# All of w_mod loaded at the start of a decode layer, the last weights behind the last V tile

## The chip, the cores and the metric

The kernel runs on one core of a Trainium2 chip. The metric is the device time of one execution in microseconds (us). Before the change it is 397.99 us, the median of three runs (397.88 to 398.57). The times in the rows further down come from one profiled execution.

## The reference

One decode step of a transformer layer for 8 sequences, all in 32-bit floats. Six vectors per sequence are computed from a conditioning input `c` and scale, shift and gate the two halves of the layer.

```
mod = (silu(c) @ w_mod).reshape(8, 6, 1, 512)
sa, ca, ga, sb, cb, gb = mod[:, 0], ..., mod[:, 5]
h = layernorm(x) * (1 + ca) + sa
q = (h @ wq)                      # 32 heads of 128, 4 heads share one of 8 KV heads
p = softmax(q k^T / sqrt(128))    # over the last 2048 of 8192 cached keys
x = x + ga * ((p v) @ wo)
h = layernorm(x) * (1 + cb) + sb
h = h @ w1 + b1                   # 512 -> 1792
x = x + gb * (relu(h)**2 @ w2 + b2)
```

## The kernel before, in words

The kernel reads some 165 MB once: 64 MiB of K, 64 MiB of V, 8 MiB each of `wq` and `wo`, 6 MiB of `w_mod`, 3.5 MiB each of `w1` and `w2` (1 MiB is 1.05 MB). All these loads are issued by one engine, SyncE (SP), in the order of the list `loads` (L144 to L152). Each goes into a slot of SBUF: two big slots (4 MiB, K tiles above all) and five small ones (2 MiB, V tiles and weights). `pump` issues the next load of the list as soon as a slot of its size is free; `done` frees one. An issue that waits holds back all those behind it, since SP works in order.

A K tile holds the 2048 keys of four sequences for one KV head; there are 16 (K0 to K15), and each head needs two. A V tile holds the values of two sequences for one head; there are 32 (V0 to V31). The main loop (L501) has one step per V tile, `s`: in a step TensorE (PE) transposes half a K tile (`transposes`, L222), multiplies the transposed keys by the queries (`scores`), and multiplies the softmax weights by a V tile that is five steps back (`weighted`, L442). VectorE (DVE) and ScalarE (ACT) copy the transposed tiles out of PSUM. Every fourth step ends a head: `soft_a` to `soft_d` do its softmax, `gather` (L471) brings the head's output into columns, and `project_o` (L486) multiplies it by the rows of `wo` for that head and adds up in `wo_ps`.

Before the loop stands the head of the program: `modulation` (L253) with the first third of `w_mod` (`modA`: sa, ca), the first layer norm, and `project_q` (L314). Of `wq` the first four heads are computed before the loop, the other four at step 4.

Behind the loop stands the tail, one long chain: `at_i` (the attention output, out of `wo_ps`), `modulation` again with the other two thirds of `w_mod` (`modB`, L117, loaded in two pieces), the residual `x1`, the second layer norm, the products with `w1` (L594), the squared relu `rT`, the products with `w2` (L614), the last two VectorE operations (L622, L623), and the output's transfer. One product that nobody reads (L611, into `spin_ps`) stands ahead of those with `w2`. The loads behind V31 are `modB`, the two biases, `w1` and `w2`.

Of the kernel before, what the change touches and what calls it, by code (L numbers as in the profile page):

```python
# [20 lines left out]
def tile_adaln_cached_attention_mlp(  # L21
# [65 lines left out]
    def size_of(key):  # L87
        return "big" if key[0] in ("K", "modB") or key == ("wo", HKV // 2 - 1) else "small"

    def load(key):  # L90
# [7 lines left out]
        if kind in "KV":  # L98


            if kind == "K":
                v = k_cache[4 * (i % 2) : 4 * (i % 2) + 4, i // 2]
            else:
                v = v_cache[i % C :: C, i // C]
            v = v[:, SK - W :, :].rearrange("u (p j) d -> p u (j d)", p=P // v.shape[0])
            nc.sync.dma_start(t, v)
            return
        if kind == "wo":

            r = 2 * REP * DH  # L110
            v = wo[i * r : (i + 1) * r, :].rearrange("(h p i) n -> p h (i n)", p=P, i=4)
        elif kind == "modA":
            v = w_mod[:, : 2 * D].rearrange(r_kc, p=P)
        elif kind == "modB":
            v = w_mod.rearrange(r_kc, p=P)
            for lo, hi in ((2, 5), (5, 6)):
                nc.sync.dma_start(  # L117
                    t[:, NQ * D * (lo - 2) : NQ * D * (hi - 2)].rearrange("p (a n) -> p a n", a=NQ),
                    v[:, :, D * lo : D * hi],
                )  # L120
            return
# [100 lines left out]
    def transposes(q, g, e):  # L222
# [30 lines left out]
    def modulation(wms, nq):  # L253

        pm = ps_m.tile([P, 512], F32, name="m_ps", tag="m_ps")
        for kc in range(NQ):
            wv = wms[kc].rearrange("p (m q n) -> p m q n", m=nq, q=NQ)
            for q in range(NQ):
                nc.tensor.matmul(
                    pm[32 * q : 32 * q + 32, : nq * P].rearrange("p (m n) -> p m n", m=nq),  # L260
                    cT[:, kc, :],
                    wv[:, :, q, :],
                    start=(kc == 0),
                    stop=(kc == NQ - 1),
                )
        return pm[:, : nq * P].rearrange("p (m n) -> p m n", m=nq)

# [16 lines left out]
    modA = consts.tile([P, 2, P], F32, name="modA")  # L284
    m = slot(("modA", 0), 2 * D)
    pm = modulation([m[:, kc, :] for kc in range(NQ)], 2)
    done(("modA", 0))
    nc.vector.tensor_copy(modA[:, 0, :], pm[:, 0, :])
    nc.vector.tensor_scalar(modA[:, 1, :], pm[:, 1, :], 1.0, None, op0=ALU.add)
# [19 lines left out]
    nc.vector.scalar_tensor_tensor(h, h, rstd, modA[:, 0, :], op0=ALU.mult, op1=ALU.add)  # L309
    hT = consts.tile([P, NQ, 32], F32, name="h1T")  # L310
    to_columns(h, hT)
    transposes(0, 1, 1)

    def project_q(r, between=()):  # L314
        pq = ps_m.tile([P, 512], F32, name="m_ps", tag="m_ps")
        for kc in range(NQ):
            w = slot(("wq", 2 * r + kc // 2), 2048)
            for g in range(4):
                nc.tensor.matmul(  # L319
                    pq[32 * g : 32 * g + 32, :],  # L320
                    hT[:, kc, :],
                    w[:, kc % 2, 512 * g : 512 * g + 512],
# [3 lines left out]
            if kc % 2:  # L326
                done(("wq", 2 * r + kc // 2))
                if between:
                    transposes(*between[kc // 2])
        qs = work.tile([P, 512], F32, name="qs", tag="a", bufs=1)  # L330
        nc.scalar.copy(qs, pq)
# [8 lines left out]
    project_q(0, ((0, 2, 0), (0, 2, 1)))  # L340
# [320 lines left out]
```

## Time and profile before

| what | value |
|---|---|
| median of three runs | 397.99 us |
| the profiled execution: its own time | 399.03 us |
| the profiled execution: span from first to last instruction | 397.2 us |
| PE busy | 327.0 us (82%) |
| DVE busy | 179.1 us (45%) |
| ACT busy | 97.0 us (24%) |
| read from HBM | 164.77 MB, 415 GB/s over the span |
| mean granted clock of TensorE | 0.974 of full speed |

The busy share is an average over the whole run. What a change is worth is read from the stage where it acts, from what each engine waits for there. "Critical chain" is the chain of work that ended last, followed back from the last instruction. The granted clock is 1.00 at 2.4 GHz and 0.50 at 1.2 GHz.

### The profile page before, as it was taken

To read this page: it belongs to the slowest core of one execution; us is meant where nothing else is said; L and a number is where in the kernel's file an instruction comes from. 1 tells how busy PE (TensorE), PEld (TensorE's weight loads), DVE (VectorE), ACT (ScalarE), POOL (GpSimd) and SP (SyncE) were. 2 spreads that over 40 slices of the span, in tenths; PEclk is the share of its full clock that TensorE was granted. 3 is DMA by queue.
4 is the path that set the end of the run, shared out by engine and by line. 5 is a ranking of instruction groups with operands and counts; after the bars stand their busy time and mean duration, and the time that the engine had idled before them with its cause. 6 is when DMAs were issued, how large, how long until landed. Compare 5 with 4: busy or idle time off the path is not lost.

```text
span 397.2 us, 6042 instructions
## 1 busy us (share of the span) xinstructions
PE 327.0 (82%) x2574; PEld 165.4 (42%) x2574; DVE 179.1 (45%) x417; ACT 97.0 (24%) x169; POOL 2.4 (1%) x12
## 2 busy tenths in 40 slices
PE   0477979796989968999869898998978789979574
PEld 0343535443444534444434444544444344533134
DVE  6142323553454435545623455555535364456320
ACT  1132224221222213123212232223122222230010
POOL 2000000000000000000000000000000000000000
PEclk9999999999899989999998999999999899989998
DMA  8999999999999999999999999999999999999992
GB/s 333 408 439 411 435 426 449 404 445 407 437 429 427 442 416 444 410 441 412 447 412 447 409 440 421 436 412 439 424 434 431 424 427 419 426 431 410 421 415 97
DMA packets 11867, 165.22 MB, mean 416 GB/s; under 512 B 1080, under 2 KB 1344, under 8 KB 3136
## 3 DMA queue, kind: packets, MB, share of 16 engines
q1 hardware_dynamic: 11696, 164.71, 97.7%
q8 instruction: 20, 0.33, 0.3%
q10 hardware_dynamic: 144, 0.13, 0.1%
q14 instruction: 7, 0.06, 0.0%
HBM read 164.77 MB, written 0.07 MB: 415 GB/s over the span
## 4 chain that ended last, share of the span: by engine, by line
DMA 44%; PE 41%; DVE 9%; ACT 4%; issue 1%; SPq 0%; ACTq 0%; DVEq 0%
DMA big<-in_A_k_cache_dram 33%; PE kt_ps L231 17%; PE s_ps L359 9%; PE o_ps L451 9%; DMA small<-in_B_w_dram 6%; DMA small<-in_w_mod_dram 4%; ACT pr L403 2%; DVE o_sb L467 2%; PE m_ps L475 2%; DVE kT L233 2%; DVE tr L479 1%; PE m_ps L614 1%; DVE pT L430 1%; PE m_ps L319 1%; PE m_ps L436 1%
## 5 line engine op out<-in xcount | busy, mean ns | idle before, releaser
L231 PE MATMUL kt_ps<-ident,big 128*128 128x128 f32 x1024 | 146.1, 286 | 45.9 <-DMA big<-in_A_k_cache_dram 35.8
L231 PEld LDWEIGHTS kt_ps<-ident,big 128*128 128x128 f32 x1024 | 113.0, 144 | 143.2 <-ACT kT L233 76.3
L233 DVE COPY kT<-kt_ps 128x512 f32<-128x512 f32 x128 | 88.3, 690 | 142.3 <-PE kt_ps L231 142.3
L233 ACT COPY kT<-kt_ps 128x512 f32<-128x512 f32 x128 | 74.8, 584 | 220.7 <-PE kt_ps L231 216.5
L359 PE MATMUL s_ps<-kT,qwin 128*32 128x512 f32 x512 | 71.5, 633 | 0.8 <-DVE qwin L345 0.8
L451 PE MATMUL o_ps<-small,pT 128*32 128x512 f32 x512 | 67.3, 603 | 0.1
L467 DVE SCALAR_TENSOR_TENSOR o_sb<-o_ps,diag,o_sb 128x128 f32<-128x128 f32 x96 | 33.7, 351 | 3.4
L465 DVE TENSOR_SCALAR o_sb<-o_ps,diag 128x128 f32<-128x128 f32 x32 | 11.2, 351 | 12.8 <-PE o_ps L451 12.8
L451 PEld LDWEIGHTS o_ps<-small,pT 128*32 128x32 f32 x512 | 11.1, 108 | 13.1 <-issue 11.6
L359 PEld LDWEIGHTS s_ps<-kT,qwin 128*32 128x32 f32 x512 | 10.4, 110 | 13.1 <-issue 11.4
L403 ACT ACTIVATE pr<-ss,nm 128x512 f32<-128x512 f32 x8 | 9.7, 1219 | 19.1 <-DVE nm L400 19.1
L427 PE MATMUL m_ps<-ident,pr 128*128 128x128 f32 x64 | 10.3, 289 | 2.2 <-DVE tr L479 2.2
L475 PE MATMUL m_ps<-o_sb,pick 128*128 128x512 f32 x16 | 9.3, 666 | 3.1 <-DVE o_sb L467 1.6
L427 PEld LDWEIGHTS m_ps<-ident,pr 128*128 128x128 f32 x64 | 7.7, 147 | 8.4 <-DVE tr L479 4.0
L430 DVE TENSOR_TENSOR pT<-m_ps,mine 128x512 f32<-128x512 f32 x16 | 10.4, 685 | 0.0
L371 DVE TENSOR_REDUCE mx<-ss 128x1 f32<-128x512 f32 x8 | 5.5, 687 | 8.6 <-ACT ss L369 8.5
L411 DVE COPY pr<-pr 128x512 f32<-128x512 f32 x8 | 3.4, 429 | 12.1 <-ACT pr L403 12.1
L319 PE MATMUL m_ps<-small,h1T 128*32 128x512 f32 x64 | 7.5, 597 | 1.5 <-DVE h1T L242 1.5
L369 ACT COPY ss<-s_ps 128x512 f32<-128x512 f32 x8 | 4.7, 587 | 11.5 <-PE s_ps L359 11.5
L479 DVE STREAM_TRANSPOSE tr<-m_ps 128x512 f32<-128x512 f32 x8 | 5.7, 717 | 2.5 <-PE m_ps L475 2.5
L614 PE MATMUL m_ps<-small,rT 128*32 128x128 f32 x112 | 4.8, 349 | 1.8 <-DMA small<-in_B_w_dram 1.8
L490 PE MATMUL wo_ps<-small,oT 128*32 128x512 f32 x48 | 6.2, 592 | 0.0
(124 smaller groups left out, 93.7 us busy)
## 6 DMA issues: line engine op xcount, KB each, us to landing
big<-in_A_k_cache_dram SPq DMA_DIRECT2D x16, 4096.0 KB, 23.6
small<-in_A_v_cache_dram SPq DMA_DIRECT2D x32, 2048.0 KB, 25.9
small<-in_A_wq_dram SPq DMA_DIRECT2D x4, 2048.0 KB, 35.4
small<-in_A_wo_dram SPq DMA_DIRECT2D x3, 2048.0 KB, 23.9
small<-in_B_w_dram SPq DMA_DIRECT2D x2, 1792.0 KB, 20.8
big<-in_w_mod_dram SPq DMA_DIRECT2D x1, 3072.0 KB, 22.5
small<-in_w_mod_dram SPq DMA_DIRECT2D x1, 2048.0 KB, 17.2
big<-in_A_wo_dram SPq DMA_DIRECT2D x1, 2048.0 KB
```

The lines of the kernel that those rows point to most:

```text
L231: nc.tensor.transpose(p[:, i, :], k[:, 32 * e + 8 * g + 4 * a + i, :], ident)
L233: (nc.vector.tensor_copy if a else nc.scalar.copy)(t[:, :, i : i + 4, :], p.rearrange("p i (r u) -> p u i r", u=4))
L319: nc.tensor.matmul(pq[32 * g : 32 * g + 32, :], hT[:, kc, :], w[:, kc % 2, 512 * g : 512 * g + 512], start=(kc == 0), stop=(kc == NQ - 1),)
L359: nc.tensor.matmul(s_ps[0][32 * u : 32 * u + 32, :], qwin[hk % 2][:, 4 * c + u, o : o + 32], kT[:, u].rearrange("p i r -> p (i r)"), start ...
L403: nc.scalar.activation(pr.rearrange("p i (r e) u -> p e i r u", e=2)[:, :, :, :, 0], SS_.pop(hk).rearrange("p (e i r) -> p e i r", e=2, i= ...
L427: nc.tensor.transpose(pp[:, i * P : (i + 1) * P], pr[:, 4 * a + i].rearrange("p r u -> p (r u)"), ident)
L430: nc.vector.tensor_mul(PT_[hk][:, a].rearrange("p x i r -> p i x r"), pp.rearrange("p (i x r) -> p i x r", i=4, r=2 * REP), mine.rearrange ...
L451: nc.tensor.matmul(o[32 * g : 32 * g + 32].rearrange("p j d -> p (j d)"), PT_[hk][:, h, 4 * c + g].rearrange("p i r -> p (i r)"), v[:, j : ...
L465: nc.vector.tensor_scalar(d, o[:, 0, :], diag[:, 0:1], None, op0=ALU.mult)
L467: nc.vector.scalar_tensor_tensor(d, o[:, j, :], diag[:, j : j + 1], d, op0=ALU.mult, op1=ALU.add)
L475: nc.tensor.matmul(pp, pick.rearrange("p t u -> p (t u)"), o.rearrange("p c d -> p (c d)"), start=True, stop=True)
L479: nc.vector.transpose(tr, pp.rearrange("p (c d i) -> p c i d", c=C, i=4))
```

## The change

The list of loads is put in another order, and the work that reads the moved weights moves with it.

- `w_mod` is loaded whole at the start, right behind K0, in four loads of 1.5 MiB (one row of 3072 values for each partition in each). `modulation` goes away: all six vectors are computed in the head of the program (two PSUM tiles, `pms`), and `ga`, `add`, `mul` and `modC` are kept for the tail.
- `wq` comes in four loads by rows instead of four blocks of columns, so all eight heads' queries are computed ahead of the loop; `turn_q` (copy, transposes, copy) stays in two parts, the second at step 1. V0 is loaded ahead of K2.
- The last `wo` rows leave their place among the last V tiles. They come behind V31 as two loads, in one big slot with the first half of `w1` (`tail`); `w2` gets the other big slot.
- `project_o` for head 6 moves from step 33 to the last step, next to head 7.
- The row of keys and values that a product takes is numbered another way (`16 * a + 4 * g` in place of `8 * g + 4 * a`), with the same shapes.
- `spin(n)` issues products that nobody reads: 1 behind the products `pw`, 1 ahead of `w1`, 3 ahead of `w2`, five in all where one stood.

```diff
+        elif kind == "mod":
+            rows(0, w_mod.rearrange(r_kc, p=P)[:, i : i + 1])
         elif kind == "wq":
-            r, half = divmod(i, 2)
-            v = wq[:, 2048 * r : 2048 * r + 2048].rearrange(r_kc, p=P)[:, 2 * half : 2 * half + 2]
+            rows(0, wq.rearrange(r_kc, p=P)[:, i : i + 1])
+        elif kind == "tail":
+            for h in range(2):
+                rows(h * 4 * D, wo_rows(HKV // 2 - 1)[:, h : h + 1])
+            rows(NJ * DH, w1v[:, 0:2])
...
-            nc.sync.dma_start(t, v)
+            for x in range(2 if key == ("V", N * 2 - 1) else 1):
+                cols = slice(x * NJ * DH // 2, (x + 1) * NJ * DH // 2) if key == ("V", N * 2 - 1) else slice(None)
+                nc.sync.dma_start(t[:, cols], v[..., cols])
...
-    loads = [("K", 0), ("modA", 0), ("wq", 0), ("wq", 1), ("K", 1), ("wq", 2), ("wq", 3), ("K", 2)]
+    loads = [("K", 0), *(("mod", k) for k in range(NQ)), *(("wq", k) for k in range(NQ)), ("K", 1), ("V", 0), ("K", 2)]
...
-    loads += [("modB", 0), ("b", 0), ("w1", 0), ("w1", 1), ("w2", 0), ("w2", 1)]
+    loads += [("b", 0), ("tail", 0), ("w1", 0), ("w2", 0)]
...
         if v >= C and v % C == 0:
-            project_o(v // C - 1)
+            for hk in {N - C: (), N: (HKV - 2, HKV - 1)}.get(v, (v // C - 1,)):
+                project_o(hk)
...
+    def spin(n):
+        for _ in range(n):
+            nc.tensor.matmul(spin_ps, ident, ident[:, None, :].to_broadcast([P, 4, P]), start=True, stop=True)
+
     at_i = work.tile([P, D], F32, name="at_i", tag="a", bufs=1)
     nc.vector.tensor_copy(at_i[:, : D // 2], wo_ps[:, : D // 2])
     nc.scalar.copy(at_i[:, D // 2 :], wo_ps[:, D // 2 :])
-    m = slot(("modB", 0), 3 * D)
-    pm = modulation([m[:, kc, :] for kc in range(NQ)], 3)
...
+    spin(1)
     x1 = consts.tile([P, P], F32, name="x1")
...
     nc.tensor.matmul(ph[:, :FG], bsel.rearrange("p g b -> p (g b)"), b1_in, start=True, stop=False)
+    spin(1)
     for kc in range(NQ):
...
-    nc.tensor.matmul(spin_ps, ident, ident[:, None, :].to_broadcast([P, 4, P]), start=True, stop=True)
+    spin(3)
     for f in range(FC):
```

SP, the last loads, before (the K tile is K15; `small` and `big` are the slots):

```order
L106 DMA big_92<-in_A_k_cache_dram 128x1x8192
L106 DMA small_95<-in_A_v_cache_dram 128x1x4096
L106 DMA small_96<-in_A_v_cache_dram 128x1x4096
L137 DMA big_91<-in_A_wo_dram 128x2x2048
L106 DMA small_93<-in_A_v_cache_dram 128x1x4096
L106 DMA small_97<-in_A_v_cache_dram 128x1x4096
L106 DMA small_94<-in_A_v_cache_dram 128x1x4096
L106 DMA small_95<-in_A_v_cache_dram 128x1x4096
L117 DMA big_92<-in_w_mod_dram 128x4x1536
L117 DMA big_92<-in_w_mod_dram 128x4x512
```

The `wo` rows stand behind V27, and V31 is followed by 4 MiB of `w_mod`.

SP, the same stretch after the change:

```order
L108 DMA big_92<-in_A_k_cache_dram 128x1x8192
L108 DMA small_93<-in_A_v_cache_dram 128x1x4096
L108 DMA small_94<-in_A_v_cache_dram 128x1x4096
L108 DMA small_96<-in_A_v_cache_dram 128x1x4096
L108 DMA small_95<-in_A_v_cache_dram 128x1x4096
L108 DMA small_97<-in_A_v_cache_dram 128x1x4096
L108 DMA small_93<-in_A_v_cache_dram 128x1x4096
L93 DMA b_in<-in_B_b_dram 4x448
L94 DMA b_in<-in_B_b_dram 4x128
L113 DMA big_91<-in_A_wo_dram 128x2048 x2
L113 DMA big_91<-in_B_w_dram 128x3584
```

Six V tiles follow K15 without a break, the last in one load, and `wo` comes behind them.

SP, the first loads before (the K tiles are K0, K1, K2 and K3):

```order
L106 DMA big_91<-in_A_k_cache_dram 128x1x8192
L137 DMA small_93<-in_w_mod_dram 128x4x1024
L137 DMA small_94<-in_A_wq_dram 128x2x2048
L137 DMA small_95<-in_A_wq_dram 128x2x2048
L106 DMA big_92<-in_A_k_cache_dram 128x1x8192
L137 DMA small_96<-in_A_wq_dram 128x2x2048
L137 DMA small_97<-in_A_wq_dram 128x2x2048
L106 DMA big_91<-in_A_k_cache_dram 128x1x8192
L106 DMA small_93<-in_A_v_cache_dram 128x1x4096
L106 DMA small_94<-in_A_v_cache_dram 128x1x4096
L106 DMA big_92<-in_A_k_cache_dram 128x1x8192
```

Ten MiB of weights stand ahead of K2, 2 MiB of them from `w_mod`.

SP, the first loads after the change (K0, K1, K2):

```order
L108 DMA big_91<-in_A_k_cache_dram 128x1x8192
L113 DMA small_93<-in_w_mod_dram 128x3072
L113 DMA small_94<-in_w_mod_dram 128x3072
L113 DMA small_95<-in_w_mod_dram 128x3072
L113 DMA small_96<-in_w_mod_dram 128x3072
L113 DMA small_97<-in_A_wq_dram 128x4096
L113 DMA small_93<-in_A_wq_dram 128x4096
L113 DMA small_94<-in_A_wq_dram 128x4096
L113 DMA small_95<-in_A_wq_dram 128x4096
L108 DMA big_92<-in_A_k_cache_dram 128x1x8192
L108 DMA small_96<-in_A_v_cache_dram 128x1x4096
L108 DMA big_91<-in_A_k_cache_dram 128x1x8192
```

Fourteen MiB of weights and V0 stand ahead of K2. Behind K2 follow V1, K3, V2, V3, K4 and so on as before.

PE, the tail before, from the products with the last V tile (`o_ps`) to those with `w2` (`rT`):

```order
L451 MATMUL o_ps<-small_95,pT 32x512 x8
L475 MATMUL m_ps<-o_sb,pick 128x512
L490 MATMUL wo_ps<-big_91,oT_137 32x512 x4
L259 MATMUL m_ps<-big_92,cT 32x384 x16
L552 MATMUL m_ps<-at_i,sel 32x128 x4
L562 MATMUL m_ps<-x1sum,sel 128x1
L259 MATMUL m_ps<-big_92,cT 32x128 x16
L584 MATMUL m_ps<-b_in,bsel 4x448
L594 MATMUL m_ps<-small_96,h2T 32x448 x8
L589 MATMUL m_ps<-ssb,ones 128x8
L594 MATMUL m_ps<-small_93,h2T 32x448 x8
```

PE, the same tail after the change:

```order
L449 MATMUL o_ps<-small_93,pT 32x512 x8
L473 MATMUL m_ps<-o_sb,pick 128x512
L489 MATMUL wo_ps<-big_91,oT_135 32x512 x4
L489 MATMUL wo_ps<-big_91,oT_136 32x512 x4
L554 MATMUL m_ps<-at_i,sel 32x128 x4
L547 MATMUL kt_ps<-ident 128x512
L565 MATMUL m_ps<-x1sum,sel 128x1
L583 MATMUL m_ps<-b_in,bsel 4x448
L547 MATMUL kt_ps<-ident 128x512
L594 MATMUL m_ps<-big_91,h2T 32x448 x8
L589 MATMUL m_ps<-ssb,ones 128x8
L594 MATMUL m_ps<-small_94,h2T 32x448 x8
```

The modulation products (`cT`) are gone from the tail, and the unread products (`kt_ps<-ident`) stand in the chain.

## Rows read from the trace of the kernel before

**Rows 1.** Busy time by stretch, end of the run; last column GB/s, PEclk granted clock.

```profile
core 0: us, PE busy (x) PEld busy (x) DVE busy (x) ACT busy (x) POOL busy (x), PEclk, DMA share, GB/s
...
392.00:392.50 0.50, 0.50 (x19) 0.50 (x14) 0.00 (x0) 0.00 (x0) 0.00 (x0) 0.62 0.04 16
392.50:394.00 1.50, 1.47 (x56) 1.21 (x46) 0.00 (x0) 0.00 (x0) 0.00 (x0) 1.00 0.00 0
```

**Rows 2.** Busy time by stretch: wq, V tiles, modB in flight.

```profile
40.00:46.00 6.00, 5.74 (x45) 3.39 (x46) 2.17 (x4) 1.75 (x3) 0.00 (x0) 1.00 1.02 423
...
345.00:359.00 14.00, 11.90 (x80) 5.09 (x72) 8.19 (x21) 4.45 (x7) 0.00 (x0) 0.88 1.00 427
364.00:372.00 8.00, 5.17 (x42) 1.11 (x34) 4.86 (x14) 0.00 (x0) 0.00 (x0) 1.00 1.02 409
```

**Rows 3.** Timeline of PE at K13 and K14: start, length, what, idle before.

```profile
290.58 1.06 PE L231 MATMUL kt_ps<-ident,big 128*128 128x128 f32 x8 [2.47 <-DMA big<-in_A_k_cache_dram]
...
310.07 1.59 PE L231 MATMUL kt_ps<-ident,big 128*128 128x128 f32 x8 [3.30 <-DMA big<-in_A_k_cache_dram]
311.59 1.93 PE L359 MATMUL s_ps<-kT,qwin 128*32 128x512 f32 x8
...
316.68 1.06 PE L359 MATMUL s_ps<-kT,qwin 128*32 128x512 f32 x8
...
324.67 1.02 PE L475 MATMUL m_ps<-o_sb,pick 128*128 128x512 f32 x2
```

**Rows 4.** Busy time by stretch, behind gaps of PE: K13, K14, last softmax.

```profile
290.00:292.00 2.00, 1.42 (x12) 1.01 (x16) 0.32 (x1) 0.58 (x1) 0.00 (x0) 1.00 1.02 434
...
310.00:312.00 2.00, 1.93 (x12) 1.42 (x16) 0.23 (x1) 0.58 (x1) 0.00 (x0) 0.62 1.00 426
...
355.00:357.00 2.00, 1.85 (x3) 0.62 (x4) 0.63 (x3) 1.82 (x3) 0.00 (x0) 0.50 1.04 442
```

**Rows 5.** Timeline of PE, last softmax and tail.

```profile
355.15 2.05 PE L475 MATMUL m_ps<-o_sb,pick 128*128 128x512 f32 x2 [1.46 <-DVE nm L400]
...
359.15 1.93 PE L451 MATMUL o_ps<-small,pT 128*32 128x512 f32 x16
...
361.75 5.68 PE L451 MATMUL o_ps<-small,pT 128*32 128x512 f32 x48
...
371.24 1.07 PE L490 MATMUL wo_ps<-big,oT 128*32 128x512 f32 x8 [1.06 <-DVE oT L480]
372.95 2.79 PE L259 MATMUL m_ps<-big,cT 128*32 128x384 f32 x32 [0.65 <-DMA big<-in_w_mod_dram]
375.56 0.40 PE L552 MATMUL m_ps<-at_i,sel 128*32 128x128 f32 x8
...
377.68 1.08 PE L259 MATMUL m_ps<-big,cT 128*32 128x128 f32 x32
378.69 1.01 PE L584 MATMUL m_ps<-b_in,bsel 4*128 4x448 f32 x2
380.00 1.71 PE L594 MATMUL m_ps<-small,h2T 128*32 128x448 f32 x16 [0.30 <-DMA small<-in_B_w_dram]
...
384.19 1.71 PE L594 MATMUL m_ps<-small,h2T 128*32 128x448 f32 x16 [2.16 <-DMA small<-in_B_w_dram]
...
386.24 1.12 PE L611 MATMUL kt_ps<-ident 128*128 128x512 f32 x2
389.17 4.80 PE L614 MATMUL m_ps<-small,rT 128*32 128x128 f32 x112 [1.80 <-DMA small<-in_B_w_dram]
```

**Rows 6.** Timeline of ACT and DVE in the tail.

```profile
372.88 0.37 ACT L541 COPY at_i<-wo_ps 128x256 f32<-128x256 f32 x1 [15.00 <-DVE at_i L540]
...
378.39 0.42 DVE L242 STREAM_TRANSPOSE h2T<-xm 128x128 f32<-128x128 f32 x1
...
387.35 0.28 DVE L606 SCALAR_TENSOR_TENSOR rT<-relu 128x112 f32<-128x112 f32 x1
```

**Rows 7.** Timeline of SP: when V30 and V31 are issued.

```profile
341.76 8.62 SPq L106 DMA_DIRECT2D small<-in_A_v_cache_dram  x2
```

More of the change, by code (lines that the diff above doesn't have):

```diff
@@ L275, in tile_adaln_cached_attention_mlp @@
     nc.vector.tensor_copy(bsel[:, :, B : 2 * B], ident[:NQ, :NQ, None].to_broadcast([NQ, NQ, B]))
-    EARLY = [(0, 0), (0, 1), (0, 2)]
-    transposes(0, 0, 0)
-    transposes(0, 0, 1)
+    EARLY = [(0, g) for g in range(4)]
     qsel = consts.tile([NQ, NQ, 32], F32, name="qsel")
     nc.vector.tensor_copy(qsel, ident[:NQ, :NQ, None].to_broadcast([NQ, NQ, 32]))
[L284 to L289, printed above, removed]
     xsum = work.tile([P, 1], F32, name="xsum")
@@ L325, in project_q, with turn_q @@
                 )
[L326 to L329, printed above, removed]
+        done(("mod", kc))
+    pm = [pms[m // 4][:, m % 4 * P : m % 4 * P + P] for m in range(6)]
+    ga, mul, add, modC = (consts.tile([P, P], F32, name=n) for n in ("ga", "mul", "add", "modC"))
+    nc.vector.scalar_tensor_tensor(h, pm[1], 1.0, h, op0=ALU.add, op1=ALU.mult)
+    nc.vector.tensor_add(h, h, pm[0])
+    hT = consts.tile([P, NQ, 32], F32, name="h1T")
+    to_columns(h, hT)
+    nc.scalar.copy(ga, pm[2])
+    nc.vector.tensor_scalar(add, pm[3], hi, None, op0=ALU.mult)
+    nc.vector.tensor_scalar(mul, pm[4], 1.0, lo, op0=ALU.add, op1=ALU.mult)
+    nc.scalar.copy(modC, pm[5])
+    pqs = [ps_m.tile([P, 512], F32, name="m_ps", tag="m_ps") for _ in range(2)]
+    for kc in range(NQ):
+        w = slot(("wq", kc), 512)
+        for r in range(2):
+            for g in range(4):
+                nc.tensor.matmul(
+                    pqs[r][32 * g : 32 * g + 32, :],
+                    hT[:, kc, :],
+                    w[:, 4 * r + g, :],
+                    start=(kc == 0),
+                    stop=(kc == NQ - 1),
+                )
+        done(("wq", kc))
+    def turn_q(r):
         qs = work.tile([P, 512], F32, name="qs", tag="a", bufs=1)
-        nc.scalar.copy(qs, pq)
+        nc.scalar.copy(qs, pqs[r])
         pT_ = ps_m.tile([P, 512], F32, name="m_ps", tag="m_ps")
@@ L486, in project_o @@
     def project_o(hk):
-        w = slot(("wo", hk // 2), D)
+        last = hk // 2 == HKV // 2 - 1
+        w = slot(("tail", 0) if last else ("wo", hk // 2), D)
         for i in range(4):
@@ L496, in project_o @@
             )
-        if hk % 2:
+        if hk % 2 and not last:
             done(("wo", hk // 2))
@@ L562, in tile_adaln_cached_attention_mlp @@
     nc.tensor.matmul(pa[:, 0:1], sel, x1sum, start=True, stop=True)
-    m = slot(("modB", 0), D)
-    pmC = modulation([m[:, 3 * NQ + kc, :] for kc in range(NQ)], 1)
     xm = work.tile([P, P], F32, name="xm", tag="one_xm", bufs=1)
```

112 lines of the change are left out of this document (41 added, 71 removed).

## The prediction

> **What bounds the kernel now.** I read the DMA rate first, then the waits of PE, then the tail. The queue of loads never runs dry: it moves 423 to 427 GB/s in mid-run and still 409 behind the loop [rows 2]. 164.77 MB at 427 would be 386 us, and the last bytes land shortly before 392.5, for the next stretch moves nothing [rows 1]. So transfers set the time, up to 4.8 us before the end of the span (397.2).
>
> PE is not far behind. It stands still for 3.30 us until K14 is there at 310.07 [rows 3], and from there to the first product with V28 at 359.15 [rows 5] nothing in the timeline waits for a load: those 49.1 us are K14, K15 and the last softmax on PE, DVE and ACT. In the tail PE waits for loads again: 0.65 us for `modB`, 0.30 and 2.16 for `w1`, 1.80 for `w2` [rows 5]. The reader is to see two chains that end almost together: the transfers, and PE from K14 on. The change takes 4 MiB out of the first behind V31 and pushes the second back by the same 4 MiB. Which of them ends last decides.
>
> **Part by part.**
>
> *Loads at the start: K14 comes 9.6 us later.* Ahead of every K tile from K2 on stand 4 MiB more. 4.19 MB at 427 GB/s are 9.8 us. Larger pieces give a little back: the 10.5 MB of `modA` and `wq` went at 423 and now go in pieces near those of V, 427 [rows 2]: 0.2 us. From V1 and K3 on the list is the old one, so each issue and the slot that it waits for move along by 9.6 us, and PE still waits before K14. The value could lie between 9.3 (all of it at the V rate and a gain on `wq` of twice that size) and 10.2 (all at the 409 of `modB`); I take 9.6, since the new pieces are larger than either old kind of `w_mod`.
>
> *Behind V31: 4 MiB less.* `modB` cost 4.19 MB at 409 [rows 2], 10.2 us; the transfers end 0.6 us earlier, near 391.9. The last `wo` rows only change their place.
>
> *From V28 to the end.* In before this took 397.25 - 359.15 = 38.1 us. Step by step [rows 5, 6]:
> - V28 to V31 and the sum into `wo_ps`: 359.15 to 372.31. Sixteen passes of V28 take 1.93 us, 1.74 without the latency, but V29 starts 2.60 us behind V28: head 6's `wo` products lie between, some 0.9. They leave the V stream and fit beside DVE's work on head 7 ahead of 371.24, where PE stands idle for 1.06. The 48 passes behind them took 5.68 where 3 x 1.74 + 0.2 are 5.4: -0.9 - 0.25, say -1.1.
> - `wo_ps` to the end of `pw`: 372.31 to 375.96, 3.65 us with `modulation` (2.79) in it. Without it the second copy ends at 373.25 [rows 6], 0.95 behind `wo_ps`, and the four products take some 0.45: 1.4 in all, -2.25.
> - `pw` to the first `w1` product: 375.96 to 380.00. DVE no longer makes `mul` and `add` ahead of `x1`. PE has a spin beside DVE's `x1`, then the bias product (1.01), then a second spin (0.95), which ends later than `h2T` does: by my estimate 3.05 instead of 4.04, so -1.0. Without the second spin `h2T` (ready at 378.81 in before [rows 6]) would decide, and it would be -1.8.
> - the `w1` products: 380.00 to 385.90, of it 2.16 for the second half, which now lands some 5 us before it is wanted: 3.5 to 3.75: -2.3.
> - `w1` to `w2`: 3.27 before, with a wait of 1.80 for `w2`. `rT` is ready 1.73 us behind the last `w1` product [rows 6], but PE first does three spins, and one such product took 1.12 alone (386.24), by my estimate 0.95 in a row, since its last 0.2 is latency: 0.4 for the bias + 2.85 = 3.25. So 0 here: what the wait gave back the spins take.
> - the `w2` products: 4.80 before, most of it at a granted clock of 0.50 (0.62 at 392.0, 1.00 behind it [rows 1]). At full clock 32 passes of the same width took 1.08 (377.68), of it some 0.2 latency, so 0.11 for four; 112 of them are 3.1, with the latency 3.25, if the spins leave no gap: -1.55.
> - the end behind them is the same.
>
> Sum: -8.2. With K14 at +9.6 the chain ends 1.4 us later than before: the span would be 398.6, if all else on the chain is as it was. Its last product would end 3.5 us behind the last load (393.97 + 1.4 against 391.9), so no load decides.
>
> *The clock.* Two stretches of the chain ran at half clock in before. K14's start: clock 0.62 on average [rows 4], its first transposes took 1.59 us against 1.06 at K13, and the scores behind them 1.93 against 1.06 at 316.68 [rows 3]; with the block that follows I take 1.6 us. And the last softmax: clock 0.50 [rows 4], `gather` 2.05 against 1.02 at K14 [rows 3, 5], some 1.0 us with the transposes behind it. What came ahead differs: a gap of 3.30 us before K14, of 1.46 before the softmax. Behind the gap of 2.47 before K13 the clock stayed at 1.00 [rows 3, 4]. So a gap of this size does not always cost the clock, and both stretches now lie 9.6 us later; I hold each of the two falls for about as likely as not.
>
> The Trainium skill, "TensorE: Matmul & The Clock Gate", section "HAM oscillation — how this bites in real kernels", says that a PE that waits for its next tile's transfer falls to the low clock and starts every such tile at half rate. The trace agrees at K14 and not at K13. By that rule K14's 1.6 us come back each time, and the sum is at least +0.4.
>
> *The rest costs nothing on the chain.* The new head (32 products of `w_mod`, eight heads of `wq`) ends when the last `wq` row has landed (18.9 MB with K0, some 47 us), and PE then has 10 us until K1. If that cover were gone, K4 would be late by what is missing, and the 3.3 us that PE stands idle before K14 would take it in. The other numbering of rows has the same shapes. V31 is issued when V26's slot is free: by 350.4 in before [rows 7], near 360 now. The loads ahead of it are fewer by the 2 MiB of `wo`, so some of the DMA queues may run out for a microsecond; V31 is wanted near 374, and only the end of the transfers, with 4 us to spare, would feel it.
>
> **The rivals.**
> - *Both half-clock stretches come back.* +1.4: 399.4. For it: 3.30 us of idle is long, and nothing in the change shortens it. Against: K13, above.
> - *Neither comes back.* 1.4 - 2.6 = -1.2 on the chain, and the last `w2` rows at 391.9 bind almost as late: 391.9 + 0.4 for the last products + 3.3 for the end are 395.6, against 396.05 by the chain. So -1.2 at most -1.6: 396.8. For it: the loads' own path really is shorter by 0.6, and with the spins the last products follow their data at full clock.
> - *The clock falls in the new tail.* It turns the result slower by itself: the `w1` or the `w2` products at half rate, priced by the rows at either level: up to 3 us on `w2`, 1.5 for a part of it, so on the likeliest case +1.5 to +3: 399.6 to 401. It decides from 1 us of loss on. For it: the gap behind the last V product at 367.4, while DVE evacuates, and two more of a microsecond. Against: before had these gaps too, at a clock of 1.00, and the spins fill the later ones.
> - *The change doesn't do all it says.* V31 is to come in halves, but the condition names tile 63, and there are 32: it is one load. That costs nothing, as V31 is early.
>
> **How the numbers follow.** The likeliest case is that one of the two half-clock stretches comes back: 1.4 - 1.6 = -0.2, or 1.4 - 1.0 = +0.4; the middle is +0.1, 398.1 (the profiled execution lay 1.0 us above the median at 399.03, and I carry the difference over to 397.99). Chance 0.42, own range 397.0 to 399.2. Both back 0.25; neither 0.18; the clock in the tail 0.10; the rest, a chain off by more than I can see, 0.05. A measurement of this kernel can tell some 0.2%, 0.8 us. My terms are good to about 0.8 us together, so of the likeliest case a tenth falls to each side; of the first rival three quarters are slower, of the second all is faster. That gives faster 0.31, same 0.37, slower 0.32. It reaches from the end of the transfers to the first rival with its error: the range 396.5 to 400.0 leaves out the worst of the tail and what lies below the end of the transfers.
>
> **What would show it right or wrong.** Right: K14 first used at 319.7 (319 to 320.5); no wait of PE for any load behind V28; the first `w2` product right behind the third spin, at a clock of 1.00; last bytes near 392. The granted clock behind K14 and in the last softmax says which case it is. Wrong: a wait for `w1` or `w2` in the tail (the chain was shorter than I think), a wait before V31, or a K14 that PE does not wait for.

## The result, and the profile after

The changed kernel takes 400.14 us, the median of 14 runs, against 398.1 us for the kernel before in the same session: a ratio of 1.005, with a 95% interval of 1.0027 to 1.0074. It is slower by some 2 us. It is also less steady: its runs lie between 398.15 and 402.58 us, those of before between 397.75 and 399.06. The profiled execution took 401.07 us (span 399.3, mean granted clock 0.965). Three runs in a much slower state (one each of e1, e14 and before, 442 to 1041 us) are left out of the ratios and ranges that follow.

The chain of waits shows what binds it. First its shares by engine (part 4 of the page), then two rows of it: start, length, what.

```profile
PE 49%; DMA 37%; DVE 9%; ACT 4%; issue 1%; SPq 0%; ACTq 0%; DVEq 0%
```

```profile
295.93 23.68 DMA big<-in_A_k_cache_dram
319.74 1.07 PE kt_ps L231 x8
```

The K14 load is the last transfer in the chain. From 319.74 to the end it holds only PE, DVE and ACT. In before PE still waited for `w1` and `w2` near the end [rows 5].

The timeline of PE, answering to [rows 3, 5], with the idle time before an instruction in brackets:

```profile
300.26 1.94 PE L231 MATMUL kt_ps<-ident,big 128*128 128x128 f32 x8 [2.51 <-DMA big<-in_A_k_cache_dram]
...
319.74 1.07 PE L231 MATMUL kt_ps<-ident,big 128*128 128x128 f32 x8 [1.86 <-DMA big<-in_A_k_cache_dram]
...
363.24 1.10 PE L473 MATMUL m_ps<-o_sb,pick 128*128 128x512 f32 x2 [1.46 <-DVE nm L398]
364.99 1.97 PE L425 MATMUL m_ps<-ident,pr 128*128 128x128 f32 x8 [0.65 <-DVE pr L409]
...
367.41 9.28 PE L449 MATMUL o_ps<-small,pT 128*32 128x512 f32 x64
378.31 1.13 PE L473 MATMUL m_ps<-o_sb,pick 128*128 128x512 f32 x2 [1.62 <-DVE o_sb L465]
...
382.11 0.87 PE L554 MATMUL m_ps<-at_i,sel 128*32 128x128 f32 x8 [0.55 <-DVE at_i L550]
...
386.08 1.71 PE L594 MATMUL m_ps<-big,h2T 128*32 128x448 f32 x16
...
390.10 2.84 PE L547 MATMUL kt_ps<-ident 128*128 128x512 f32 x6
392.87 3.27 PE L613 MATMUL m_ps<-big,rT 128*32 128x128 f32 x112
```

K14 is first used at 319.74, 9.7 us later than before. Nothing behind it waits for a load, and the `w2` products follow the third spin directly and take 3.27 us. So far this is the forecast. The surprise is the row at 367.41: the 64 passes of V28 to V31 take 9.28 us. Busy time by stretch, answering to [rows 1, 4] (the granted clock is the third number from the end of a row):

```profile
319.00:321.00 2.00, 1.26 (x12) 1.01 (x16) 0.51 (x3) 0.55 (x1) 0.00 (x0) 1.00 1.04 442
...
365.00:367.00 2.00, 2.00 (x9) 1.63 (x9) 1.60 (x5) 0.97 (x2) 0.00 (x0) 0.50 0.95 402
367.00:369.00 2.00, 2.00 (x10) 0.79 (x14) 0.80 (x2) 0.00 (x0) 0.00 (x0) 0.50 1.00 418
369.00:371.00 2.00, 2.00 (x16) 0.57 (x12) 0.00 (x0) 0.00 (x0) 0.00 (x0) 0.50 1.03 433
...
390.00:392.00 2.00, 2.00 (x7) 0.95 (x6) 1.29 (x4) 0.00 (x0) 0.00 (x0) 1.00 0.12 45
392.00:394.00 2.00, 2.00 (x46) 1.24 (x48) 0.00 (x0) 0.00 (x0) 0.00 (x0) 1.00 0.00 0
```

At K14 the clock stayed at 1.00. From 365 to 371 us it was 0.50 (1.2 GHz), in the last softmax and in half of the V products behind it. The transfers were over before 392.

### The profile page after: what moved, and what is told of

Same layout as the page of the kernel before. It is cut to its first block, busy times and chain, and to the rows that moved or that the text cites. A ratio compares the mean times of both kernels' runs of the same rounds, so it can differ in the third digit from the quotient of the medians.

```text
span 399.3 us, 5987 instructions
## 1 busy us (share of the span) xinstructions
PE 334.1 (84%) x2550; PEld 165.0 (41%) x2550; DVE 178.5 (45%) x416; ACT 97.4 (24%) x169; POOL 2.5 (1%) x12
## 4 chain that ended last, share of the span: by engine, by line
PE 49%; DMA 37%; DVE 9%; ACT 4%; issue 1%; SPq 0%; ACTq 0%; DVEq 0%
DMA big<-in_A_k_cache_dram 27%; PE kt_ps L231 19%; PE o_ps L449 11%; PE s_ps L357 9%; DMA small<-in_A_wq_dram 6%; DMA small<-in_w_mod_dram 4%; ACT pr L401 2%; DVE o_sb L465 2%; PE m_ps L473 2%; DVE kT L233 2%; DVE tr L477 1%; PE kt_ps L547 1%; PE m_ps L293 1%; DVE pT L428 1%; DVE pr L409 1%
## 5 line engine op out<-in xcount | busy, mean ns | idle before, releaser
L357 PE MATMUL s_ps<-kT,qwin 128*32 128x512 f32 x512 | 70.1, 622 | 0.8 <-DVE qwin L343 0.8
L449 PE MATMUL o_ps<-small,pT 128*32 128x512 f32 x512 | 69.1, 620 | 0.0
L318 PE MATMUL m_ps<-small,h1T 128*32 128x512 f32 x64 | 11.1, 829 | 10.3 <-DMA small<-in_A_wq_dram 10.3
L473 PE MATMUL m_ps<-o_sb,pick 128*128 128x512 f32 x16 | 8.4, 604 | 3.1 <-DVE o_sb L465 1.6
L333 DVE COPY qall<-m_ps 128x128 f32<-128x128 f32 x2 | 0.8, 390 | 21.4 <-PE m_ps L332 21.4
L318 PEld LDWEIGHTS m_ps<-small,h1T 128*32 128x32 f32 x64 | 2.1, 134 | 18.9 <-DMA small<-in_A_wq_dram 9.8
L293 PE MATMUL m_ps<-small,cT 128*32 128x512 f32 (+1 forms) x64 | 6.0, 492 | 2.0 <-DMA small<-in_w_mod_dram 2.0
```

What stands on the lines that cost most here:

```text
L293: nc.tensor.matmul(pm[32 * q : 32 * q + 32, : (m1 - m0) * P].rearrange("p (m n) -> p m n", n=P), cT[:, kc, :], wv[:, m0:m1, q, :], start=( ...
L318: nc.tensor.matmul(pqs[r][32 * g : 32 * g + 32, :], hT[:, kc, :], w[:, 4 * r + g, :], start=(kc == 0), stop=(kc == NQ - 1),)
L357: nc.tensor.matmul(s_ps[0][32 * u : 32 * u + 32, :], qwin[hk % 2][:, 4 * c + u, o : o + 32], kT[:, u].rearrange("p i r -> p (i r)"), start ...
L449: nc.tensor.matmul(o[32 * g : 32 * g + 32].rearrange("p j d -> p (j d)"), PT_[hk][:, h, 4 * c + g].rearrange("p i r -> p (i r)"), v[:, j : ...
L473: nc.tensor.matmul(pp, pick.rearrange("p t u -> p (t u)"), o.rearrange("p c d -> p (c d)"), start=True, stop=True)
```

## The experiments

Theory 1: with the change, the chain of PE, DVE and ACT from K14 to the end has no slack, so each half-clock stretch on it adds to the time, where before most of them passed while PE would have waited for loads. Rivals: the loads still bind; the order of the last V and `wo` loads costs; the added spins pay for themselves. Each is timed against before in the same session (398.0 to 398.3 us):

| run | median us | ratio to before, 95% interval |
|---|---|---|
| e1_no_spin3 | 398.40 | 1.0000 [0.9986, 1.0014] |
| e2_warm_softmax | 400.56 | 1.0054 [1.0033, 1.0075] |
| e3_before_wo_last | 398.55 | 1.0008 [0.9999, 1.0018] |
| e4_late_mod | 397.74 | 0.9996 [0.9981, 1.0010] |
| e6_warm_k14 | 400.75 | 1.0057 [1.0026, 1.0087] |
| e7_warm_all | 401.15 | 1.0083 [1.0051, 1.0115] |
| e9_late_mod_warm | 397.39 | 0.9984 [0.9974, 0.9994] |
| e10_warm_head | 399.60 | 1.0035 [1.0023, 1.0047] |
| e11_warm_all2 | 398.20 | 0.9999 [0.9990, 1.0008] |
| e12_head_delay | 402.64 | 1.0108 [1.0083, 1.0132] |
| e13_warm_no_spin3 | 397.02 | 0.9971 [0.9960, 0.9982] |
| e14_warm_head_k14 | 398.39 | 1.0018 [1.0002, 1.0034] |
| e15_before_warm | 397.98 | 0.9995 [0.9986, 1.0004] |

### Is it the chain, and which part?

**e1**, the changed kernel without the three spins ahead of `w2`:

```diff
-    spin(3)
```

> The changed kernel without the three unread products ahead of w2. Theory 1 (PE's chain from K14 to the end binds, and these products lie on it): rT is ready 1.7 to 1.8 us behind the last w1 product, in the changed kernel the w2 products started 3.1 us behind it; so 1.2 to 1.4 us less, a median near 398.8. Rival (the products hold the clock, and pay for themselves): the w2 products, 3.27 us at full clock, fall to half rate, some 6 us, and the time stays at 400 or rises.

398.40 us, 1.7 less than the changed kernel: the products lie on the chain, and the loads do not bind. From the last `w1` products to `w2` its trace gives 3.49 us (387.51 to 391.00) in place of 4.83 (388.04 to 392.87), so 1.3 of it is theirs.

**e3**, before with only the new place of the last `wo` rows:

```diff
-            if v % (2 * C) == 2 * C - 4:
+            if v % (2 * C) == 2 * C - 4 and v < 6 * C:
...
+    loads += [("wo", HKV // 2 - 1), ("modB", 0),
...
+            for hk in {N - C: (), N: (HKV - 2, HKV - 1)}.get(v, (v // C - 1,)):
+                project_o(hk)
```

> The kernel before with two edits of the change alone: the last wo rows loaded behind V31 (in one piece), and head 6's wo products next to head 7's. w_mod stays as before, so K14 is there at 310 and 4 MiB of w_mod follow behind wo. Theory 1: PE's chain is ahead of the loads, the loads set the end, 398.1 (397.5 to 398.7), with the narrow spread of before. Rival (the new order of the last V tiles and wo is what costs): 399 or more.

398.55: no cost that can be told. That rival falls. The other new parts (`wq` by rows, all queries ahead of the loop, the other numbering of rows) were not run by themselves; they all stand in e4 and in e11 and e13 below, which are no slower than before.

**e4**, the changed kernel with 4 MiB of `w_mod` taken back out of the start. They are loaded ahead of V28, and their products stand in the last softmax:

```diff
+    loads = [("K", 0), ("mod", 0), *(("wq", k) ...
+            if v == 7 * C:
+                loads.append(("modB", 0))
...
             soft_c(g - 1)
+            if s == N + 1:
+                modB_products()
```

> The changed kernel with w_mod in two parts again: sa and ca (2 MiB) at the start, the other 4 MiB between V27 and V28 in one load of 8 KB pieces, their products in the last softmax's idle time of PE. K14 is at 310 again, V31 lands near 369.6 as in the changed kernel, the loads behind it stay 9 MiB. Theory 1: PE waits for V31 and then for w1 and w2, the loads set the end near 391.9, and with the products ahead of w2 at full clock the end is 0.4 + 3.3 behind it: span 395.6 to 396, median 397.4 to 397.8, narrow spread. Rival (the five unread products or the tail's own length cost): 399 or more.

397.74, 2.4 below the changed kernel. So the loss hangs on the 4 MiB ahead of K14. In its trace K14 is at 309.72 again, and the last V tile becomes the wait that counts:

```profile
370.06 2.82 PE L469 MATMUL o_ps<-small,pT 128*32 128x512 f32 x16 [3.00 <-DMA small<-in_A_v_cache_dram]
```

**e2**, the changed kernel with products nobody reads in the gap of the last softmax. `heat` is used in all that follow; `heat(4)` is one product of 512 columns:

```diff
+    def heat(*cols):
+        wm = ps_kt.tile([P, 4, P], F32, name="kt_ps")
+        for u in cols:
+            nc.tensor.matmul(wm[:, :u], ident, ident[:, None, :].to_broadcast([P, u, P]), start=True, stop=True)
...
+        if hk == HKV - 1:
+            heat(4, 2)
         nm = work.tile([P, 1], F32, name="nm")
```

> The changed kernel with one unread product of 512 columns and one of 256 behind the second small product of the last softmax, where PE stood idle for 1.46 us. Theory 1 with its clause on the clock: the half-clock stretch in the last softmax and the V products (364.7 to 371.5 in the changed kernel's trace) goes, the V28 to V31 products take 7.1 instead of 9.3 us; the profiled span near 396.7 if K14 keeps its clock too, the median 398.5 to 399.2, the spread of the runs about half of 4.4. Rival (the loads bind, or everything is only later by the 4 MiB): no change, 400.1.

400.56: no gain, a miss. In its trace the softmax ran at full clock, but now K14 did not (PE timeline, then busy time by stretch):

```profile
319.43 1.94 PE L231 MATMUL kt_ps<-ident,big 128*128 128x128 f32 x8 [3.30 <-DMA big<-in_A_k_cache_dram]
```

```profile
319.00:323.00 4.00, 3.57 (x17) 1.85 (x18) 0.69 (x1) 0.59 (x1) 0.00 (x0) 0.57 1.00 426
361.00:367.00 6.00, 4.83 (x23) 2.09 (x24) 3.61 (x12) 2.52 (x4) 0.00 (x0) 1.00 0.97 400
```

One stretch is not the whole loss. Nor does the gap of 1.46 us decide it: e1, e10, e12 and e14 have the same gap in the last softmax, and there the V products took 7.24 or 7.25 us. In e10:

```profile
364.50 1.10 PE L479 MATMUL m_ps<-o_sb,pick 128*128 128x512 f32 x2 [1.46 <-DVE nm L404]
...
368.15 7.25 PE L455 MATMUL o_ps<-small,pT 128*32 128x512 f32 x64
```

### Warming more of the chain, clumsily

**e5**, before once more, for its trace:

> The kernel before, unchanged, profiled once more, to see which part of its path made the first profiled execution (399.03 us) 1.0 us longer than the median. Theory A (the last products at half clock made it: the granted clock was 0.50 from 389.0 us on, and the 112 w2 products took 4.80 us): an execution of about 398.0 us shows the w2 products at a clock of 1.00 in 3.3 to 3.8 us, the last loads again near 392.5 us and K14 at its place near 310; the forecast then counted this microsecond twice, once as the w2 term and once when it went from the profiled execution to the median. Theory B (the loads were slower as a whole): the last loads land about 1 us earlier and the w2 products look as before.

398.48 us. The `w2` products were again at half clock, so theory A was not shown here; but K14 came 0.4 us earlier than in the first profile (310.07 [rows 3]), which is part of theory B. PE timeline:

```profile
309.68 1.90 PE L231 MATMUL kt_ps<-ident,big 128*128 128x128 f32 x8 [3.31 <-DMA big<-in_A_k_cache_dram]
...
354.79 1.10 PE L475 MATMUL m_ps<-o_sb,pick 128*128 128x512 f32 x2 [1.46 <-DVE nm L400]
...
358.44 1.93 PE L451 MATMUL o_ps<-small,pT 128*32 128x512 f32 x16
...
388.79 4.64 PE L614 MATMUL m_ps<-small,rT 128*32 128x128 f32 x112
```

e15 below comes back to it.

**e6**, `heat(4, 4, 4, 4)` ahead of the first transposes of K13 and K14; **e7**, the same with e2's edit and `heat(4, 4, 4)` ahead of the last `gather`:

```diff
+        if h == 0 and q in (13, 14):
+            heat(4, 4, 4, 4)
         if s < N and (q, 2 * h) not in EARLY:
             transposes(q, 2 * h, 0)
```

> The changed kernel with four unread 512-column products ahead of the first transposes of K13 and of K14, where PE waited 2.5 and 1.9 us in the profiled run (3.3 in others): about 1.9 us of work inside each wait. [...] Rival (the falls do not come from these waits, or come back at the next gap): median 400.1 as the changed kernel. Rival 2 (the products delay K14): 400.5 and more.

> As the one before, with unread products also in the last softmax (768 columns, as in e2) and behind the last V product, where PE waits 1.62 us for DVE (three of 512 columns). Theory 1: without a gap above 1 us between K13 and the w1 products the clock stays at 1.00, the runs lie within about 1 us of each other near the changed kernel's lowest, 398.2 to 398.8, and the mean clock is higher by 0.01. Rival (the clock falls in this kernel whatever PE does in these gaps): 400 to 400.6 with a spread of 4 us, as e2.

400.75 and 401.15: the edits were too long. I had taken 0.47 us for such a product, but that is one of its two passes. The trace of e6:

```profile
317.77 3.70 PE L267 MATMUL kt_ps<-ident 128*128 128x512 f32 x8
321.31 0.93 PE L231 MATMUL kt_ps<-ident,big 128*128 128x128 f32 x7
```

Four of them took 3.70 us, and K14, which PE took up at 319.4 to 319.7 in the traces of the changed kernel and of e2, began at 321.31. Rival 2 of e6 held. As a test of theory 1 both runs are void.

**e9**, e4 without `spin(3)`, with four unread products of 512 columns ahead of K13 and of K14, five ahead of the last V tile and three behind the last V product:

> A version put together from what the first four showed: the changed kernel with the last two thirds of w_mod loaded late (as e4), without the three products ahead of w2 (as e1), and with unread products in PE's waits for K13, K14 and the last V tile and behind the last V product. Theory 1: the chain is then shorter than the loads, so that the end of the transfers (near 392 us) decides again: 397.0 to 397.4 with a spread below 1 us, 0.2% below before. Rival (the added products delay the chain, or the clock falls all the same): 397.7 or more, spread as e4's 2.6 us.

397.39, and nine of its 12 runs lie within 0.4 us: the version beats before by 0.16%. The other three lie 1.2 to 1.4 us above the median, and the profiled one (398.78) is of these. In it the added products did not fit: the five ahead of the last V tile ran partly at half clock, and the tile's products began at 372.82, against 370.06 in e4:

```profile
368.09 4.79 PE L271 MATMUL kt_ps<-ident 128*128 128x512 f32 x10
372.82 1.92 PE L475 MATMUL o_ps<-small,pT 128*32 128x512 f32 x16
```

### The head of the program

In the trace of e1 K14 was first used at 321.78, 2.0 us later than in the changed kernel's own. Something ahead of it had held up the transfers. Busy time by stretch, the changed kernel and then e1 (last column GB/s):

```profile
75.00:80.00 5.00, 4.65 (x38) 2.43 (x31) 2.83 (x5) 1.75 (x4) 0.00 (x0) 1.00 1.12 472
80.00:85.00 5.00, 3.59 (x29) 2.16 (x27) 1.89 (x6) 3.50 (x5) 0.00 (x0) 1.00 0.97 419
```

```profile
75.00:80.00 5.00, 4.41 (x33) 2.58 (x32) 2.67 (x4) 2.47 (x5) 0.00 (x0) 1.00 0.97 347
80.00:85.00 5.00, 5.00 (x40) 2.67 (x38) 1.94 (x5) 2.39 (x4) 0.00 (x0) 1.00 0.92 370
```

Theory 2: from 49 us on PE works off K0 and K1 without a wait for a load until 73.7 us; if it is late there, the slots come free late, SP issues late, and every later tile lands late. Two experiments, one warming PE among the `wq` rows (**e10**), one holding it up by 2.8 us behind them (**e12**):

```diff
     for kc in range(NQ):
+        heat(*([4] * (4 if kc == 0 else 2)))
         w = slot(("wq", kc), 512)
```

```diff
         done(("wq", kc))
+    heat(4, 4, 4)
```

> The changed kernel with unread 512-column products ahead of each wq row's products, four ahead of the first and two ahead of the others, inside PE's waits there (4.9, 1.2, 1.3 and 3.0 us in its profile). From 49 us on PE works without a pause for over 20 us until K0 and K1 are done, and SP issues the next K and V loads when it gives their slots back; in the e1 execution a half-clock stretch at 50 to 57 us was followed by a pause of 2.3 us in the transfers near 80 us, and every later tile, K14 too (321.8 instead of 319.7), came 2 us later. Theory 2 (part of the loss comes from the head: half clock there starves the transfers): no half clock from 45 to 60 us, K14 at 319.4 to 319.8 in the profiled execution, the median 0.5 to 1.2 us lower, 399.0 to 399.7. Theory 1 alone (only the clock behind K14 counts): 400.1, as the changed kernel.

> The changed kernel with three unread 512-column products (2.8 us) behind the last wq product, where the prediction said that PE has 10 us until K1 and that a delay would be taken in by PE's waits before K14. If the prediction was right there: same as the changed kernel, 400.1. Theory 2 (the slots of K0 and the V tiles come free when PE is done, so that a late PE stops the transfers): a pause of the transfers of some 2 us near 80 us, K14 lands 2 to 3 us later, and the time is 2 to 3 us longer, 402.1 to 403.1.

e10: 399.60, 0.5 less than the changed kernel. The intervals of the two overlap, so this gain is not shown; what changed clearly is the spread, 0.65 us in place of 4.4 (all five runs between 399.20 and 399.85). e12: 402.64, 2.5 more. SP (issue of K2, which waits for K0's slot), the changed kernel and then e12:

```profile
56.08 0.54 SPq L108 DMA_DIRECT2D big<-in_A_k_cache_dram  x1
```

```profile
60.44 0.54 SPq L108 DMA_DIRECT2D big<-in_A_k_cache_dram  x1
```

The trace of e12 has the pause, 282 GB/s from 75 to 80 us, and K14 starts at 323.01:

```profile
75.00:80.00 5.00, 4.76 (x39) 2.56 (x39) 2.07 (x3) 1.77 (x4) 0.00 (x0) 1.00 0.74 282
```

```profile
323.01 1.94 PE L231 MATMUL kt_ps<-ident,big 128*128 128x128 f32 x8 [3.29 <-DMA big<-in_A_k_cache_dram]
```

So most of a delay of PE in the head reaches the end. In this execution, the slowest of e12's (404.66), the last `wq` row was at half clock as well (3.60 us against 1.92); with that and the added products K2 was issued 4.4 us later and K14 used 3.3 us later. Of the medians, 2.8 us put in came out as 2.5, by the two intervals give or take 1.4. In e10's trace the head and the last softmax were at full clock; only K14 was not, and for K1, behind the head, PE waited 0.25 us (busy time by stretch, then PE timeline):

```profile
45.00:60.00 15.00, 11.97 (x85) 4.89 (x78) 2.35 (x5) 2.24 (x4) 0.00 (x0) 1.00 1.01 430
319.00:323.00 4.00, 3.53 (x17) 1.79 (x17) 0.69 (x1) 0.58 (x1) 0.00 (x0) 0.57 1.03 438
365.00:371.00 6.00, 5.08 (x40) 2.07 (x42) 3.49 (x10) 2.21 (x4) 0.00 (x0) 1.00 1.00 422
```

```profile
59.47 1.06 PE L231 MATMUL kt_ps<-ident,big 128*128 128x128 f32 x8 [0.25 <-DMA big<-in_A_k_cache_dram]
```

### All of it, in sizes that fit

**e11**, e10 with `heat(4, 4)` ahead of K13 and K14, e2's edit, and `heat(4, 2)` ahead of the last `gather`; **e13**, the same without `spin(3)`; **e14**, e11 without the last two edits:

> e10 with further unread products that fit inside PE's waits this time (in e7 the four ahead of K14 took 3.7 us and held K14 up by 1.2): two of 512 columns ahead of K13 and of K14, 768 columns in the last softmax, 768 behind the last V product. Theory 1 and 2 together: no half clock in the head, nor from 300 us to the w2 products; runs near the changed kernel's lowest, 398.1 to 398.7, with a spread of about 1 us. Rival (the loss has another source): 399.5 or more.

> e11 without the three products ahead of w2, which in e1 were worth 1.7 us. Theory 1 and 2: 396.8 to 397.4, the chain then ends about where the loads allow (392 us and 3.5 behind it), 0.2 to 0.3% below before. Rival (the loss has another source, or the clock falls for want of the three products): 398.4, as e1, or more.

> e10 with two unread 512-column products ahead of the first transposes of K13 and of K14, and nothing in the last softmax nor behind the last V product. If the 1.4 us between e10 and e11 are K14's alone: as e11, 398.2, no half clock from 319 to 323 us. If the clock then falls in the last softmax instead, as in the changed kernel's own profile: 2.6 us more than e11 in the runs where it does, 399.5 to 401 and a wide spread.

e11: 398.20, all 11 runs between 397.99 and 398.44. Of a spread of 4.4 us 0.45 is left, and the median is 1.9 us below that of the changed kernel, though nothing was taken out and 36 passes of PE were put in. Its trace at K14 and in the last V products (PE timeline):

```profile
319.50 1.07 PE L231 MATMUL kt_ps<-ident,big 128*128 128x128 f32 x8 [1.38 <-DMA big<-in_A_k_cache_dram]
...
366.63 7.25 PE L457 MATMUL o_ps<-small,pT 128*32 128x512 f32 x64
```

e13: 397.02 (396.94 to 397.16), 0.3% below before and the best of all. `rT` now decides when the `w2` products start, with no spin between:

```profile
388.50 3.62 PE L624 MATMUL m_ps<-big,rT 128*32 128x128 f32 x112 [1.36 <-DVE rT L618]
```

e14: 398.39. Six of its ten runs lie between 398.26 and 398.39, two at 399.0, and two at 400.45 and 400.85, 2.25 and 2.65 above e11. Most of the 1.4 us between e10 and e11 is K14's. By their size the two slowest runs fit the softmax stretch, which would then come seldom here; they have no trace, so this is argued, not shown.

**e15**, the same protection for the kernel before (K13, K14, softmax, last `gather`, and its own waits for `w1` and `w2`):

```diff
+            heat(4, 4)
             rstd = work.tile([P, B], F32, name="rstd_b")
...
-    nc.tensor.matmul(spin_ps, ident, ident[:, None, :].to_broadcast([P, 4, P]), start=True, stop=True)
+    for _ in range(2):
+        nc.tensor.matmul(spin_ps, ident, ident[:, None, :].to_broadcast([P, 4, P]), start=True, stop=True)
```

> The kernel before with unread products in its waits: two of 512 columns ahead of K13 and of K14, 768 columns in the last softmax and behind the last V product, two of 512 in the wait for the second half of w1, and a second one ahead of w2. Theory 1 and 2 (in before a half-clock stretch of PE only takes up time in which PE would wait for loads, but for the last one, in the w2 products behind the last loads): 397.2 to 397.9, 0.2 to 0.9 us below before. At full clock the changed kernel (e11, 398.2) is then slower than before by 0.3 to 1.0 us, about what its three products ahead of w2 cost. Rival (before gains nothing, it ends with the loads at any clock): 398.0.

397.98, as before (the rival's number, at the upper end of theory 1's): before had almost nothing to win. In its trace the `w2` products ran at full clock and waited for their data; K14 had come at 310.19, as late as in the first profile of before:

```profile
310.19 1.06 PE L231 MATMUL kt_ps<-ident,big 128*128 128x128 f32 x8 [1.38 <-DMA big<-in_A_k_cache_dram]
...
389.29 1.96 PE L627 MATMUL m_ps<-small,rT 128*32 128x128 f32 x64 [0.97 <-DMA small<-in_B_w_dram]
391.65 1.71 PE L627 MATMUL m_ps<-small,rT 128*32 128x128 f32 x48 [0.41 <-DMA small<-in_B_w_dram]
```

With these stretches at full clock, then, the two kernels stand at 398.20 and 397.98: the moved work nearly balances, and of the 2 us that the change costs some 1.9 are the clock (400.14 against 398.20).

## Why the prediction was wrong, point by point

The forecast was 398.1 us, no change; the time is 400.14, just outside the range. The chain from K14 binds, no load behind it does, and the clock decides: that much was right. Two sizes failed, and one step, the cover for the head, was wrong. Of the 2.0 us by which the forecast missed, 1.4 lie in the time without any half-clock stretch (396.8 in the rival "neither comes back", 398.20 in e11), and 0.6 in what the clock adds to it (1.3 forecast, 1.9 measured).

- *K14 9.6 us later:* 9.7 (319.74 against 310.07 [rows 3]). Right.
- *The loads end near 391.9, and PE waits for none behind V28:* right.
- *`pw` to `w1` 3.05, the `w1` products 3.5 to 3.75, three spins so that `w2` starts 3.25 behind, the `w2` products 3.25:* measured from the rows of PE 3.1 (382.98 to 386.08), 3.67 (to 389.75), 3.12 (to 392.87) and 3.27. Each within 0.15.
- *Sum of the terms, -8.2 + 9.6:* with both half-clock stretches gone the working gives 399.03 - 1.2 = 397.8 for the profiled execution. e11's profiled execution, at full clock from K14 on, took 398.25: 0.45 off, and the price of the softmax stretch below is more than that.
- *"The profiled execution lay 1.0 us above the median at 399.03, and I carry the difference over to 397.99":* the first failed step. Some 0.6 of it was before's `w2` products at half clock: with K14 equally late they ended at 393.97 there (389.17 + 4.80 [rows 5]) and at 393.36 in e15 at full clock. The term for `w2` had already taken that out, so it was counted twice. The other 0.4 was the loads: in e5, the same kernel, K14 came 0.4 earlier (309.68) and the `w2` products, at half clock too, ended at 393.43. This is read from three executions; in e11 the profiled one lies 0.05 above its median, not 1.0.
- *"The last softmax: clock 0.50, ... some 1.0 us":* the second failed step, a mis-sized term. In the changed kernel's trace the stretch covered not only `gather` and the transposes but also V28 and V29. From the first transposes of K14 to the end it was 399.3 - 319.74 = 79.6 us there and 396.5 - 319.50 = 77.0 in e11: 2.6. The rows say where: 9.28 against 7.25 for the V products, 1.97 against 1.41 for the transposes. In before, on the other hand, it had cost less than 1.0: from `gather` to the first product with V28 PE took 4.00 us (355.15 to 359.15 [rows 5]) and 3.65 in e5, where the clock stayed at 1.00. So 0.35 was all that its absence could give back in that execution, and the longer `gather` only took up time in which PE waited for DVE. Put right in these two places (0.6 and 0.65), 396.8 becomes 398.05, against 398.20 for e11.
- *K14's stretch, 1.6 us:* right in size. In e10, with that stretch alone, K14 to the end took 398.0 - 319.47 = 78.5, 1.5 more than in e11. It is not always so: in e12 the clock came back some 7 us after K14's start, and from there to V28 PE took 50.0 (323.01 to 373.03) against 47.1 in e11 (319.50 to 366.63), 2.9 more.
- *"One of the two comes back":* with the sizes as measured this is 398.2 + 1.5 = 399.7 or 398.2 + 2.6 = 400.8, and the median of 400.14 lies between. The 14 runs, from 398.15 to 402.58, would fit none, one or both; only one of them has a trace, so that reading of the others is argued, not shown. It also leaves out a third source, the head (next point). e2, with the softmax filled, still spreads over 4.1 us, and seven of its ten runs lie above 400, more than the 399.7 that K14's stretch alone would give; e10, with the head filled and nothing else, spreads over 0.65 in five runs. So the head is the likeliest source of the spread, and of e2's miss; that too is argued.
- *"PE then has 10 us until K1 ... the 3.3 us that PE stands idle before K14 would take it in":* wrong, and not in any rival. In these 10 us PE works on K0. In e10, where the head was at full clock, 0.25 us of waiting for K1 was left, in the changed kernel none. And the wait before K14 is a wait for a load, which comes late when the slots come free late. e12 showed it: K2 issued 4.4 us late, K14 used 3.3 late, with a wait of 3.29 ahead of it all the same.
- *"I hold each of the two falls for about as likely as not", with K13 as the case against K14:* K13 and K14 hang together. In the changed kernel's trace K13's transposes ran at half clock (1.94 at 300.26), PE was later by that, its wait ahead of K14 was 1.86 in place of 3.3, and K14 started at full clock. In e2 and e10, where the wait was 3.3, K14 did not.
- *"The clock falls in the new tail":* the `w1` and `w2` products kept their clock in all traces of the changed kernel and of its versions (1.71 us for each half of `w1`). The loss was one stage earlier.

The Trainium skill, "TensorE: Matmul & The Clock Gate", section "HAM oscillation — how this bites in real kernels", describes a kernel whose PE waits some 3 to 5 us for each next tile's transfer and starts every such tile at the low clock. The waits of 3.3 us ahead of K14 agree with it in seven traces (before, e2, e3, e4, e5, e10, e12); the waits of 1.86 here and of 1.38 in e11 are shorter, and the clock stayed at 1.00. One of 3.29 us ahead of K6 in e1 does not agree, as the clock behind it was 1.00:

```profile
154.30 1.07 PE L231 MATMUL kt_ps<-ident,big 128*128 128x128 f32 x8 [3.29 <-DMA big<-in_A_k_cache_dram]
```

Nor does the length of the wait alone decide it: the wait for K13 was 2.51 us in the changed kernel and in e2, and its transposes took 1.94 us in the first (the row at 300.26 above) and 1.06 in e2:

```profile
299.94 1.06 PE L231 MATMUL kt_ps<-ident,big 128*128 128x128 f32 x8 [2.51 <-DMA big<-in_A_k_cache_dram]
```

What else decides it is open.

## What to carry to other kernels

A stretch at half clock cost next to nothing where PE would have waited for transfers anyway (e15 against before: 0.1 us) and all the time that it added once the chain of engines bound (e11 against the changed kernel: 1.9 us). So a change that moves the bound from loads to PE has to be priced with the clock as it falls in the new order, and its runs spread. Put unread products into PE's waits, but measure one first and keep them shorter than the wait; where they outlast it they lie on the chain (the three ahead of `w2`: 1.2 us between e11 and e13). A number in which the profiled execution differs from the median may be carried over only after one knows which stage made it.

## What the runs showed of the hardware that was not expected

- An unread 128x512 product in 32-bit floats is two passes and took 0.93 us in a row (3.70 for four).
- A half-clock stretch can go on while PE is busy: behind gaps of 1.46 and 0.65 us it held from 365 to 371 us. The same gaps in e1, e10, e12 and e14 left the clock at 1.00.
- With all the larger gaps filled in parts, the mean granted clock rose from 0.965 to 0.996 in the profiled execution of e11, and the spread of the runs fell from 4.4 to 0.45 us.
